# Two row tiles to one key/value instruction, with a newly stored order, in a fused attention and gated-MLP kernel

## The chip, the cores and the metric

The kernel runs on one core of one Trainium2 chip. The metric is the device time of one execution in microseconds, as the median of several runs; lower is better. One more execution is recorded by the hardware profiler, and everything said of instructions below comes from that record. The notes call the engines PE (TensorE, matrix products), ACT (ScalarE), DVE (VectorE), POOL (GpSimd) and SP (SyncE, which here issues nearly all DMAs).

## The reference

Input x has 2048 rows of 448 numbers in bf16. All weights are bf16.

```python
x = A_x
h  = x + _A_ref(_layernorm(x), A_wqkv, A_w_phi, A_wo)
h2 = h + _B_ref(_layernorm(h), B_w_gate, B_w_up, B_w_down)

# _A_ref: 16 heads of 28
q, k, v = split(x @ wqkv)
phi_q = concat(softmax(q @ w_phi), softmax(-(q @ w_phi)))
phi_k = concat(softmax(k @ w_phi), softmax(-(k @ w_phi)))
kv  = einsum("bhsf,bhsd->bhfd", phi_k, v)
z   = sum over s of phi_k
num = phi_q @ kv ;  den = phi_q @ z + 1e-6
out = (num / den) @ wo
# _B_ref
out = (sigmoid(x @ w_gate) * (x @ w_up)) @ w_down      # w_gate, w_up: 448 x 1792
```

The state kv is a sum over all 2048 rows, so every row's keys and values must be done before the first row's num can start.

## The kernel before

**Tiles.** The rows are 16 tiles of 128. The work goes by these tasks, named as in the code with the tile, pair or chunk behind the name:

- First layer norm, by tile: statistics `bst`, `agg`; the root `rstd` on POOL; the normalized tile `xn` on DVE or ACT. The transposed tile `xT` comes from PE for tiles 0 to 3 and from a DMA transpose of two tiles for the rest (line 628, issued by SP).
- Weights folded with w_phi: for keys `kT`, `WkT`, `wM1`, `W21` at the start; for queries two DMA transposes `wqT` (line 508), then `wM0` (line 562) and `W20`.
- Keys and values (line 644): one pair of products of 448 columns each takes turns on the two halves of PE's rows. It is two tasks, a first part of four steps (`pa`) and a second of three (`pb`), and fills one pair of PSUM banks. Before the change a pair is the keys and the values of one tile, for all tiles but the first two.
- Softmax of the keys, by tile: `ekp` and `ekm` (exponentials of both signs, ACT, lines 664 and 666), `v1` (values out of PSUM, ACT or DVE), `ss` (sums, DVE, line 685), `rs` (reciprocals, DVE, line 689), `phi` (the product, DVE or POOL, line 691). Then `kv` (PE, line 703) adds the tile to the state in bank 4, and `kvz` (DVE, line 758) takes the state out after tile 15.
- Queries by chunks of four tiles and two halves of the heads: `qa` and `q` (PE, line 743), `eqp` and `eqm` (ACT, line 753).
- Attention by tile: `num` (PE, line 779), `ocp` (ACT or DVE, out of PSUM). By pair of tiles on DVE: `rSm`, `rr`, `b`, `c`, `rd`, `o`, `od` (lines 795 to 826). The transpose `oT` is on PE for pair 0 and a DMA for the others. `woa` and `wo_` (PE, line 840) are the output product. For pair 0 the residual is added on PE (`wr`), and `hc`, `bst2`, `agg2` read PSUM; for the others `h` (line 870) adds it on DVE. Then `ve2`, `rstd2` (POOL, line 880), `hn` (DVE, line 884), `hP` and `hT`.
- MLP by chunks of 2, 4, 4, 4 and 2 tiles: `ga` and `gu` (PE, line 941, gate and up together), `sig` (ACT, line 950), `hh` (DVE, line 958), `dn` (PE, line 975), `fin` (DVE, line 982), `st` (the store, line 985). Tile 15 alone is split into two halves of 224 columns, `dn` 15 and `dn` 15,1.

**What sets the order.** Every task is one entry of a graph with its needs. The table ORDER holds, for every task, its number, its choice among the PSUM banks and its choice of engine. The tasks are issued on their engines in the order of the table, and each engine runs its own queue strictly in that order:

```python
for v in table.split():
    t = self.tasks[names[int(v) // 32]]
    t.eng = t.engs[int(v) % 4]
    ...
        t.got, gate = t.banks[int(v) // 4 % 8]
        for b in t.got:
            t.need += bank_until.get(b, [])
```

So a product whose banks were used before waits for the readers of their former content (`until`). Keys and values may use the bank pairs 0-1, 2-3 and 6-7. A second table, TURNS, adds needs by hand: an entry `(name, first)` makes `name` wait for `first` as well. Nearly all entries hold a POOL task back until a DVE task is done. A few products of zeros (`warm`, `fill`) run on PE while the first loads are under way.

Of the kernel before, what the change touches and what calls it, by code (L numbers as in the profile page):

```python
# [11 lines left out]
D = 448  # L12
H = 16
DH = 28
# [18 lines left out]
NFILL = 12  # L33
# [56 lines left out]
TURNS = [(('rstd', 4), ('xn', 3)), (('phi', 0), ('xn', 9)), (('phi', 4), ('xn', 12)), (('phi', 7), ('xn',  # L90
         15)), (('phi', 10), ('phi', 9)), (('phi', 14), ('phi', 13)), (('ve2', 2), ('hn', 3)), (('rstd2', 2),
         ('hn', 3)), (('ve2', 4), ('o', 5)), (('rstd2', 4), ('o', 5)), (('rstd2', 3), ('od', 5)), (('rstd2',
         5), ('od', 7))]
# [7 lines left out]
class _Graph:  # L101
# [29 lines left out]
    def opt(self, name):  # L131
        return name if name in self.tasks else None
# [180 lines left out]
def act_p(n):  # L313
    return 0.05 + n / 1200.0
# [14 lines left out]
def build(nc, A_x, A_wqkv, A_w_phi, A_wo, B_w_gate, B_w_up, B_w_down, out):  # L329
# [19 lines left out]
    with ExitStack() as es:  # L349
# [236 lines left out]
        VV = (0,)  # L586
        batches = [(0, 1), (1, 2), (2, 4), (4, 8), (8, 12), (12, 16)]
        for (a, z) in batches:
# [13 lines left out]
            for t in range(a, z):  # L602
                s = t % NXP
                free = opt(("xT", t - NXP if t - NXP in PE_X else (t - NXP) // 2 * 2))

                def f(e, t=t, s=s):
                    dst, src = xn_pad[:, s, :].rearrange("p (a n) -> p a n", a=2), lap(X(t))
                    if K.tasks[("xn", t)].eng == "act":
                        return e.activation(dst, src, ACT.Identity, bias=nm1[:, t:t + 1], scale=rs1[:, t:t + 1])
                    return e.tensor_scalar(dst, src, mv1[:, t, 0:1], rs1[:, t:t + 1], op0=ALU.subtract, op1=ALU.mult)  # L610
                task(("xn", t), None, dve(160), f, [("rstd", a), opt(("nm", a)), free],
                     engs=("dve",) if a < 4 else ("act", "dve"))
# [37 lines left out]
        for t in range(NT):  # L650
            if t in VV:
                both_ = [xT_of[t], xT_of[t + 1]]
                pair_of(("va", t), ("vb", t), [(t, Wv), (t + 1, Wv)], both_ + WV, [("v1", t), ("v1", t + 1)])
                pair_of(("pa", t), ("pb", t), [(t, Wk2), (t + 1, Wk2)], both_ + WK2,
                        [(n, u) for n in ("ekp", "ekm") for u in (t, t + 1)])
# [6 lines left out]
        for t in range(NT):  # L662
            s = t % NEK
            task(("ekp", t), "act", act_p(D), lambda e, t=t, s=s: e.activation(  # L664
                ek[:, s, 0, :], bank[got(k_at[t][0])[k_at[t][1]]][:, 0:D], ACT.Exp), [k_at[t][2], opt(("phi", t - NEK))])
            task(("ekm", t), "act", act_p(D), lambda e, t=t, s=s: e.activation(  # L666
                ek[:, s, 1, :], bank[got(k_at[t][0])[k_at[t][1]]][:, 0:D], ACT.Exp, scale=-1.0),
                [k_at[t][2], opt(("phi", t - NEK))])
            task(("v1", t), None, act_p(D), lambda e, t=t: copy(
                e, v1[:, t % NV, :, 0:DH], bank[got(v_at[t][0])[v_at[t][1]]][:, 0:D].rearrange("p (h d) -> p h d", d=DH)),  # L670
# [365 lines left out]
```

## Time and profile before

| what | value |
|---|---|
| median of 3 runs | 205.62 us (205.51 to 205.68) |
| the profiled execution | 205.42 us |
| its span, first to last instruction | 203.7 us |
| PE busy in the span | 195.8 us |
| DVE, ACT, POOL busy | 134.2, 94.6, 32.8 us |
| DMA | 16.94 MB |
| granted TensorE clock, mean | 0.999 |

The span is 1.7 us shorter than the execution that it is part of. "Busy" of PE is modelled from the starts of pipelined products, so two that overlap count once. A wait is put down to the instruction that released it.

### The profile page before, as it was taken

What the parts mean: (1) busy time and instruction counts of PE and PEld (TensorE: products, weight loads), DVE (VectorE), ACT (ScalarE), POOL (GpSimd) and SP (SyncE); (2) the same over time, 40 slices, a digit from 0 to 9 for tenths busy, and PEclk for the clock granted to TensorE, in tenths of its full rate; (3) what the DMA queues carried; (4) which work ended last, traced back from release to release, by engine and by line L of the source; (5) the groups of instructions that cost most, each with busy time, mean ns of one, the idle gap of its engine ahead of it and who ended that gap; (6) DMA issues with size and microseconds to landing.
All of it is one profiled execution on the core that took longest, in us unless ns stands there. A gap on an engine that the chain in (4) does not pass through costs nothing.

```text
span 203.7 us, 5394 instructions
## 1 busy us (share of the span) xinstructions
PE 195.8 (96%) x2276; PEld 109.5 (54%) x2276; DVE 134.2 (66%) x304; ACT 94.6 (46%) x169; POOL 32.8 (16%) x51
## 2 busy tenths in 40 slices
PE   7997999998889999999999999999999999999994
PEld 2543546555446985554445555454444555786553
DVE  2979989897999995789949846722455313541412
ACT  2699999999999553344031441202224400442000
POOL 5516936660000200003000100110000000000000
PEclk9999999999999999999999999999999999999999
DMA  5999696653045283501250020050020000200141
GB/s 144 313 271 149 173 194 159 187 198 93 3 103 145 80 93 79 140 0 43 51 116 3 0 53 3 5 121 3 0 74 3 2 3 0 69 3 0 34 158 59
DMA packets 35109, 16.94 MB, mean 83 GB/s; under 512 B 26828, under 2 KB 34060, under 8 KB 35084
## 3 DMA queue, kind: packets, MB, share of 16 engines
q1 hardware_dynamic: 34812, 16.36, 33.5%
q8 instruction: 18, 0.29, 0.6%
q10 hardware_dynamic: 272, 0.23, 0.3%
q14 instruction: 7, 0.06, 0.1%
HBM read 8.98 MB, written 1.84 MB: 53 GB/s over the span
## 4 chain that ended last, share of the span: by engine, by line
PE 86%; DMA 5%; DVE 3%; SPq 3%; issue 1%; ACT 0%; DVEq 0%
PE bank L941 42%; PE bank L975 21%; PE bank L644 8%; PE bank L743 5%; PE bank L840 5%; DMA WqT<-wq_raw 3%; SPq L468 3%; PE bank L703 2%; DMA wq_raw<-in_A_wqkv_dram 2%; PE bank L779 1%; SPq L508 1%; DVE o_pad L807 1%; DVE opm L432 1%; DVE st L865 1%; PE bank L562 1%
## 5 line engine op out<-in xcount | busy, mean ns | idle before, releaser
L941 PE MATMUL bank<-xnT,wu_sb 64*128 64x512 bf16 (+1 forms) x490 | 87.6, 333 | 0.0
L941 PE MATMUL bank<-xnT,wg_sb 64*128 64x512 bf16 (+1 forms) x490 | 87.5, 333 | 0.0
L950 ACT ACTIVATE sg_sb<-bank 128x512 f32<-128x512 f32 (+1 forms) x70 | 34.6, 511 | 81.4 <-PE bank L941 75.6
L958 DVE SCALAR_TENSOR_TENSOR hh<-sg_sb,bank 128x512 bf16<-128x512 f32 (+1 forms) x70 | 39.0, 575 | 30.3 <-ACT sg_sb L950 28.0
L941 PEld LDWEIGHTS bank<-xnT,wg_sb 64*128 64x128 bf16 x490 | 45.0, 94 | 20.8 <-issue 2.8
L941 PEld LDWEIGHTS bank<-xnT,wu_sb 64*128 64x128 bf16 x490 | 44.8, 94 | 13.9
L975 PE MATMUL bank<-wd_sb,hh 128*128 128x448 bf16 (+1 forms) x238 | 43.1, 342 | 0.0
L975 PEld LDWEIGHTS bank<-wd_sb,hh 128*128 128x128 bf16 x238 | 22.9, 98 | 20.1 <-DVE hh L958 0.4
L982 DVE SCALAR_TENSOR_TENSOR x_sb<-bank,x_sb 128x448 bf16<-128x448 f32 (+1 forms) x17 | 9.8, 594 | 24.6 <-PE bank L975 24.5
L644 PE MATMUL bank<-Wv,xnT 64*128 64x448 bf16 x112 | 21.9, 350 | 0.1
L644 PE MATMUL bank<-Wk,xnT 64*128 64x448 bf16 x112 | 21.7, 350 | 0.2
L691 POOL TENSOR_TENSOR phi<-ek,rsum 128x896 bf16<-128x896 bf16 x10 | 16.8, 1688 | 8.9 <-DVE xn_pad L610 4.7
L685 DVE TENSOR_REDUCE ssum<-ek 128x32 f32<-128x896 bf16 x16 | 16.6, 1069 | 0.8 <-ACT ek L664 0.7
L753 ACT ACTIVATE eq<-bank 128x1024 bf16<-128x1024 f32 x16 | 16.6, 1062 | 0.2
L880 POOL TENSOR_TENSOR rs<-rs,neghalf 128x2 f32<-128x2 f32 x8 | 5.6, 698 | 59.5 <-DVE rs L878 59.2
L743 PE MATMUL bank<-xnT,Wq 64*128 64x512 bf16 x112 | 14.3, 377 | 0.0
L840 PE MATMUL bank<-wo_sb,oT 64*128 64x448 bf16 x112 | 13.0, 350 | 0.6 <-DVE rs L878 0.6
L432 ACT CAST opm<-bank 128x960 bf16<-128x960 f32 x13 | 12.0, 972 | 1.4 <-PE bank L779 1.4
L644 PEld LDWEIGHTS bank<-Wk,xnT 64*128 64x128 bf16 x112 | 9.2, 94 | 5.9 <-PE bank L644 1.5
L644 PEld LDWEIGHTS bank<-Wv,xnT 64*128 64x128 bf16 x112 | 9.2, 94 | 5.0 <-ACT WkT L432 0.4
L870 DVE TENSOR_TENSOR x_sb<-bank,x_sb 128x896 bf16<-128x896 f32 x7 | 7.5, 1087 | 3.4 <-PE bank L840 3.4
L666 ACT ACTIVATE ek<-bank 128x448 bf16<-128x448 f32 x16 | 8.9, 563 | 0.9 <-PE bank L644 0.9
(92 smaller groups left out, 168.0 us busy)
## 6 DMA issues: line engine op xcount, KB each, us to landing
wu_sb<-in_B_w_up_dram SPq DMA_DIRECT2D x4, 448.0 KB, 4.1
wg_sb<-in_B_w_gate_dram SPq DMA_DIRECT2D x4, 448.0 KB, 3.9
out_dram<-x_sb SPq DMA_DIRECT2D x15, 112.0 KB, 1.8
wd_sb<-in_B_w_down_dram SPq DMA_DIRECT2D x7, 224.0 KB, 2.8
x_sb<-in_A_x_dram SPq DMA_DIRECT2D x2, 448.0 KB, 4.8
x_sb<-in_A_x_dram SPq DMA_DIRECT2D x3, 224.0 KB, 4.4
wq_raw<-in_A_wqkv_dram SPq DMA_DIRECT2D x4, 128.0 KB, 3.7
Wv<-in_A_wqkv_dram SPq DMA_DIRECT2D x2, 224.0 KB, 4.8
```

The costliest lines, as they stand in the source:

```text
L432: return e.copy(dst, src) if hasattr(e, "activation") else e.tensor_copy(dst, src)
L644: r = e.matmul(bank[bk][:, 0:D], lhsT=half(xnT, hi)[:, t, k, :], rhs=half(w, hi)[:, k, :], start=(i == 0), stop=(i == 6), tile_position=(6 ...
L685: task(("ss", t), "dve", dve(896), lambda e, s=s: e.tensor_reduce(ssum[:, s, :].rearrange("p (a h) -> p a h", h=2), ek[:, s].rearrange("p ...
L691: task(("phi", t), None, 1.68, lambda e, t=t, s=s: e.tensor_tensor(phi[:, t % NPHI, :, :, 0:DH, :].rearrange("p a g d h -> p (a g) d h"), ...
L743: r = e.matmul(bank[bb[j]], lhsT=half(Wq2, hi)[:, k, 2 * g:2 * g + 2].rearrange("p c d h -> p (c d h)"), rhs=half(xnT, hi)[:, 4 * c:4 * c ...
L753: task((key, gp, c), "act", act_p(1024), lambda e, gp=gp, c=c, sg=sg, nm=nm: e.activation(eq[c][:, sg, 2 * gp:2 * gp + 2, :], wide[got(nm) ...
L840: r = e.matmul(bank[bb[j]][:, 0:D], lhsT=half(oT, hi)[:, pr % NO, j, k, :], rhs=half(wo_sb, hi)[:, k, :], start=(i == 0 and not res), stop ...
L941: r = e.matmul(bank[b][:, 0:N], lhsT=half(w, hi)[:, k, fs], rhs=half(hnT, hi)[:, t0:t0 + n, k, :], start=(i == 0), stop=(i == 6), tile_pos ...
L950: task(("sig", f_, c), "act", act_p(N), lambda e, j=j, N=N, nm=nm: e.activation(sg_sb[:, j % NSG, 0:N], bank[got(nm)[0]][:, 0:N], ACT.Tanh ...
L958: task(("hh", f_, c), "dve", dve(N), lambda e, j=j, N=N, nm=nm, f_=f_, c=c: e.scalar_tensor_tensor(hhT[c % 2][:, f_, 0:N], sg_sb[:, j % NS ...
L975: r = e.matmul(bank[b][:, c0:c1], lhsT=hhT[c % 2][:, f_, o:o + P], rhs=wd_sb[:, f_, c0:c1], start=(f_ == 0), stop=(f_ == FT - 1))
L982: task(("fin",) + nm[1:], "dve", dve(c1 - c0), lambda e, nm=nm, tt=tt, pr=pr, c0=c0, c1=c1: e.scalar_tensor_tensor(X(tt)[:, c0:c1], bank[g ...
```

## The change

Keys and values are no longer paired within a tile. For every two tiles t and t+1 (t even) there is one pair of products with the values of both (`va`, `vb`) and one with the keys of both (`pa`, `pb`), as tiles 0 and 1 had it before. Where t is in PAIRED (2 to 12, that is tiles 2 to 13), one instruction over both banks does `ekp` for two tiles, one does `ekm`, one `v1`, one `ss`, one `rs`. `phi` and `kv` stay by tile, and tiles 0, 1, 14 and 15 stay single. A bank pair is now free when the one reader of both banks is done. Two needs that named `pb` by number now look the task up (`k_at`), and the unused branch SPLIT is gone. There are 14 fill products in place of 12.

ORDER is a new table for the whole program, and TURNS has 7 entries in place of 12. Cut to its core:

```diff
-NFILL = 12
+NFILL = 14
-TURNS = [(('rstd', 4), ('xn', 3)), (('phi', 0), ('xn', 9)), (('phi', 4), ('xn', 12)), (('phi', 7), ('xn',
-         15)), (('phi', 10), ('phi', 9)), (('phi', 14), ('phi', 13)), (('ve2', 2), ('hn', 3)), (('rstd2', 2),
-         ('hn', 3)), (('ve2', 4), ('o', 5)), (('rstd2', 4), ('o', 5)), (('rstd2', 3), ('od', 5)), (('rstd2',
-         5), ('od', 7))]
+TURNS = [(('phi', 3), ('phi', 2)), (('phi', 5), ('xn', 14)), (('phi', 8), ('phi', 9)), (('rstd2', 0), ('c',
+         3)), (('rstd2', 2), ('hn', 3)), (('rstd2', 4), ('od', 5)), (('rstd2', 6), ('hn', 10))]
...
-        VV = (0,)
+        VV = tuple(range(0, NT, 2))
+        PAIRED = (2, 4, 6, 8, 10, 12)
...
+                def keys(t=t, n=n):
+                    nm, j, _ = k_at[t]
+                    return wide[got(nm)[0]][:, j:j + n, 0:D]
+                task(("ekp", t), "act", act_p(n * D), lambda e, s=s, n=n, keys=keys: e.activation(
+                    ek[:, s:s + n, 0, :], keys(), ACT.Exp), [k_at[t][2]] + free)
+                task(("ekm", t), "act", act_p(n * D), lambda e, s=s, n=n, keys=keys: e.activation(
+                    ek[:, s:s + n, 1, :], keys(), ACT.Exp, scale=-1.0), [k_at[t][2]] + free)
+                task(("v1", t), None, act_p(n * D), lambda e, t=t, n=n: copy(
+                    e, v1[:, t % NV:t % NV + n, :, 0:DH],
+                    wide[got(v_at[t][0])[0]][:, v_at[t][1]:v_at[t][1] + n, 0:D].rearrange("p c (h d) -> p c h d", d=DH)),
...
+                task(("ss", t), "dve", dve(896 * n), lambda e, s=s, n=n: e.tensor_reduce(
+                    ssum[:, s:s + n, :].rearrange("p c (a h) -> p (c a) h", h=2),
+                    ek[:, s:s + n].rearrange("p c a (g d h) -> p (c a g) h d", g=2 * G, h=2), AX.X, ALU.add),
+                task(("rs", t), "dve", dve(256 * n), lambda e, s=s, n=n: e.reciprocal(rsum[:, s:s + n, :], ssum[:, s:s + n, :]),
```

What the new ORDER makes of the queues, where it differs most:

- SP: x of tiles 0 to 7 and the key weights first, as before; then the query weights `wq` stand ahead of the value weights `wv`, with x of tiles 8 to 11 between the `wq`; x of tiles 12 to 15 still stands last before the two transposes `wqT`.
- PE, first stage: the four `kT` stand together, the key products of tiles 0 to 3 come before the value products. From `wM0` on, pairs of `va` and `pa` alternate; `kv` goes two or three tiles at a time.
- After `kvz`: `num` 0, 2, 1, 4, 3, 6, 5, 7 among the queries of chunks 2 and 3; `ocp` 0 and 1 on DVE and 2 to 7 on ACT (before 0 and 3 on DVE).
- Pair 0 of the second layer norm: both `hc` are on DVE (before one was on ACT). The DVE queue is `hc` 1, `bst2` 0, `b` 3, `bst2` 1, `hc` 0, the two `agg2`, `c` 3, `h` 1, `hn` 1, `hn` 0, `h` 2, `hT`. `rstd2` 0 on POOL waits for `c` 3 (TURNS). On PE `woa` 2 and `wo_` 2 now stand ahead of `hP`. Fourteen `num` stand before the first `ga` (before: thirteen).
- The end of PE's queue is `dn` 10, 12, 11, 14, 15, 15,1, 13; before it was `dn` 12, 10, 13, 14, 11, 15, 15,1.

More of the change, by code (lines that the diff above doesn't have):

```diff
@@ L603, in build @@
                 s = t % NXP
-                free = opt(("xT", t - NXP if t - NXP in PE_X else (t - NXP) // 2 * 2))
+                free = None if t < NXP else ("xT", t - NXP if t - NXP in PE_X else (t - NXP) // 2 * 2)
                 def f(e, t=t, s=s):
@@ L652, in build @@
                 both_ = [xT_of[t], xT_of[t + 1]]
-                pair_of(("va", t), ("vb", t), [(t, Wv), (t + 1, Wv)], both_ + WV, [("v1", t), ("v1", t + 1)])
+                pair_of(("va", t), ("vb", t), [(t, Wv), (t + 1, Wv)], both_ + WV, [("v1", u) for u in ((t,) if t in PAIRED else (t, t + 1))])
                 pair_of(("pa", t), ("pb", t), [(t, Wk2), (t + 1, Wk2)], both_ + WK2,
-                        [(n, u) for n in ("ekp", "ekm") for u in (t, t + 1)])
+                        [(n, u) for n in ("ekp", "ekm") for u in ((t,) if t in PAIRED else (t, t + 1))])
                 for j in range(2):
@@ L663, in build @@
             s = t % NEK
[L664 to L670, printed above, removed]
-                [v_at[t][2], "v1one", opt(("kv", t - NV))], engs=("act", "dve"))
@@ L673, in build @@
-            if t in SPLIT:
-                task(("sa", t), None, 0.88, lambda e, t=t, s=s: e.tensor_tensor(
-                    half_s[:, t % NSA].rearrange("p (a n) -> p a n", a=4 * G),
-                    ek[:, s].rearrange("p a (g n) -> p (a g) n", g=2 * G)[:, :, 0:DH],
-                    ek[:, s].rearrange("p a (g n) -> p (a g) n", g=2 * G)[:, :, DH:2 * DH], ALU.add),
-                    [("ekp", t), ("ekm", t), opt(("ss", t - NSA))],
-                    engs=("pool", "dve"))
-                task(("ss", t), "dve", dve(448), lambda e, t=t, s=s: e.tensor_reduce(
-                    ssum[:, s, :].rearrange("p (a h) -> p a h", h=2),
-                    half_s[:, t % NSA].rearrange("p (a d h) -> p a h d", a=4 * G, h=2), AX.X, ALU.add),
-                    [("sa", t), opt(("rs", t - NEK))])
-            else:
-                task(("ss", t), "dve", dve(896), lambda e, s=s: e.tensor_reduce(
-                    ssum[:, s, :].rearrange("p (a h) -> p a h", h=2),
-                    ek[:, s].rearrange("p a (g d h) -> p (a g) h d", g=2 * G, h=2), AX.X, ALU.add),
-                    [("ekp", t), ("ekm", t), opt(("rs", t - NEK))])
@@ L689, in build @@
-            task(("rs", t), "dve", dve(256), lambda e, s=s: e.reciprocal(rsum[:, s, :], ssum[:, s, :]),
-                 [("ss", t), opt(("phi", t - NEK))])
+            n = 2 if t in PAIRED else 1
+            if t - 1 in PAIRED:
+                pass
+            else:
+                free = [opt(("phi", u - NEK)) for u in range(t, t + n)]
+                def keys(t=t, n=n):
[8 more added lines that the diff above has]
+                    wide[got(v_at[t][0])[0]][:, v_at[t][1]:v_at[t][1] + n, 0:D].rearrange("p c (h d) -> p c h d", d=DH)),
+                    [v_at[t][2], "v1one"] + [opt(("kv", u - NV)) for u in range(t, t + n)], engs=("act", "dve"))
+                task(("ss", t), "dve", dve(896 * n), lambda e, s=s, n=n: e.tensor_reduce(
+                    ssum[:, s:s + n, :].rearrange("p c (a h) -> p (c a) h", h=2),
+                    ek[:, s:s + n].rearrange("p c a (g d h) -> p (c a g) h d", g=2 * G, h=2), AX.X, ALU.add),
+                    [("ekp", t), ("ekm", t), opt(("rs", t - NEK)), opt(("rs", t - NEK + 1))])
+                task(("rs", t), "dve", dve(256 * n), lambda e, s=s, n=n: e.reciprocal(rsum[:, s:s + n, :], ssum[:, s:s + n, :]),
+                     [("ss", t)] + free)
@@ L691, in build @@
+            of = t - 1 if t - 1 in PAIRED else t
             task(("phi", t), None, 1.68, lambda e, t=t, s=s: e.tensor_tensor(
@@ L694, in build @@
                 rsum[:, s, :].rearrange("p (a h) -> p a h", h=2)[:, :, None, :].to_broadcast([P, 4 * G, DH, 2]), ALU.mult),
-                [("rs", t), ("ekp", t), ("ekm", t), opt(("kv", t - NPHI))], engs=("dve", "pool"))
+                [("rs", of), ("ekp", of), ("ekm", of), opt(("kv", t - NPHI))], engs=("dve", "pool"))
             def f(e, t=t):
@@ L707, in f @@
                 return r
-            task(("kv", t), "pe", 0.28, f, [("phi", t), ("v1", t), opt(("kv", t - 1)) or "kv0"], pace=1.9, rows=127)
+            task(("kv", t), "pe", 0.28, f, [("phi", t), ("v1", of), opt(("kv", t - 1)) or "kv0"], pace=1.9, rows=127)
         task("kv0", "pe", 0.22, lambda e: e.matmul(
@@ L718, in build @@
                  deps=([late[i - 2][0]] if i > 1 else []) + [
-                     ("kvz" if j < 4 else ("gu", 1 + 2 * j, 0)) if name[0] == "wd" else ("pb", 4 + 2 * j + (name[0] == "wu"))])
+                     ("kvz" if j < 4 else ("gu", 1 + 2 * j, 0)) if name[0] == "wd" else k_at[4 + 2 * j + (name[0] == "wu")][2]])
         WO_MOVES = [(0, 0, 112, 0, 0), (1, 0, 16, 0, 112), (1, 16, 96, 1, 0), (2, 0, 32, 1, 96), (2, 32, 80, 2, 0),
@@ L747, in build @@
                 deps = WQ2 + [xT_of[t] for t in range(4 * c, 4 * c + 4)]
-                deps.append(("pb", min(4 * c + 3, NT - 1)))
+                deps.append(k_at[min(4 * c + 3, NT - 1)][2])
                 task(nm, "pe", pes(4, 512), lambda e, f=f: f(e, steps=range(4)), deps,
@@ L887, in build @@
                     [("rstd2", pr), h_of.get(t)] + [d for d in hT_of.get(pr - NHP, [])])
-            qdone = [("q", gp, c) for gp in range(2)] + [("pb", NT - 1)]
+            qdone = [("q", gp, c) for gp in range(2)] + [k_at[NT - 1][2]]
             if pr in PE_O:
```

91 rows, old and new, of the table ORDER are left out of this document.

## The prediction

> **What bounds the kernel now.** I read the page's first part, then busy time by stages that I cut at the places where the kind of work changes, then PE's waits in each stage, and last the chain and the DMA view at both ends of the program.
>
> ```profile
> PE 195.8 (96%) x2276; PEld 109.5 (54%) x2276; DVE 134.2 (66%) x304; ACT 94.6 (46%) x169; POOL 32.8 (16%) x51
> ...
> core 0: us, PE busy (x) PEld busy (x) DVE busy (x) ACT busy (x) POOL busy (x), PEclk, DMA share, GB/s
> ...
> 6.50:18.10 11.60, 10.34 (x106) 5.46 (x106) 10.14 (x32) 10.81 (x24) 4.53 (x10) 1.00 1.15 256
> 18.10:46.50 28.40, 28.40 (x498) 15.90 (x500) 26.36 (x51) 26.41 (x50) 18.30 (x14) 1.00 0.70 175
> 46.50:64.80 18.30, 16.17 (x330) 8.83 (x330) 17.38 (x41) 17.62 (x22) 0.70 (x1) 1.00 0.35 92
> 64.80:77.60 12.80, 12.77 (x252) 11.29 (x245) 11.99 (x35) 6.96 (x17) 1.58 (x3) 1.00 0.54 85
> 77.60:184.70 107.10, 107.09 (x997) 57.09 (x998) 60.72 (x127) 30.78 (x57) 3.68 (x6) 1.00 0.14 35
> 184.70:200.80 16.10, 16.05 (x99) 9.40 (x98) 4.42 (x10) 0.76 (x4) 0.00 (x0) 1.00 0.21 66
> 200.80:203.70 2.90, 0.00 (x0) 0.00 (x0) 0.38 (x1) 0.00 (x0) 0.00 (x0) 0.91 0.24 72
> ```
>
> From 18.1 us on PE is the bound, at the full clock. In the key/value stage (18.1 to 46.5) it has no idle time at all, although ACT and DVE are at 93% there, and from 64.8 to 200.8 it misses 0.09 us. What can be won or lost lies in four places: how early PE can start its unbroken run (18.1), whether ACT and DVE still keep up until 46.5, the 2.13 us idle between 46.5 and 64.8, and the 2.9 us behind PE's last product. The change leaves the number of products as it was (two more fills run while PE waits for loads), so PE's own work cancels in the difference.
>
> PE's waits between 46.5 and 64.9, and the chain at the start and end:
>
> ```profile
> PE bank L779 <- DVE opm L432: 0.6, 2, 0.5
> PE bank L848 <- DVE oT L432: 0.6, 1, 0.6
> PE bank L840 <- DVE rs L878: 0.6, 1, 0.6
> PE bank L779 <- ACT opm L432: 0.3, 1, 0.3
> ...
> 10.50 1.39 SPq L508
> ...
> 12.00 6.05 DMA WqT<-wq_raw
> 18.05 0.05 issue
> 18.10 0.77 PE bank L562 x12
> ...
> 184.72 16.05 PE bank L975 x98
> 200.76 0.02 issue
> 200.79 0.39 DVE x_sb L982
> ```
>
> **a. The start.** PE's run begins when the second query transpose lands. The new SP queue puts the `wq` loads ahead of `wv`, so the transposes can be issued earlier than 10.50. But their packets stand behind all loads issued before them, and the bytes ahead are the same but for 84 KB (a 98 KB piece of `wo` gives way to one of 14 KB). The DMA engines run full from 6.5 to 16.6 (share 1.15). At the 256 GB/s of that stage 84 KB are 0.3 us. The view of 16 to 18 us, in 40 slices of 50 ns, shows one thing more:
>
> ```profile
> GB/s 231 225 174 251 195 210 230 195 195 128 118 51 31 15 0 0 0 0 0 10 5 10 10 5 10 10 10 10 5 15 5 15 5 10 26 246 266 297 297 287
> ...
> q8 instruction: 1, 0.02, 1.6%
> ```
>
> For about 1.1 us, from 16.6 to 17.7, nearly nothing moves, and only then does the transpose end. The second row, of the view of 12 to 16 us, is a read of instructions just ahead of it. Whether it falls there again cannot be read from the trace; PE's instruction count reaches that point at about the same time. I take -0.3 us, with bounds of -1.0 (the gap goes) and +0.3.
>
> **b. The key/value stage.** The 18 merged ACT instructions each replace two. Their pitch, start to start, and that of a longer one:
>
> ```profile
> 30.42 0.55 ACT L666 ACTIVATE ek<-bank 128x448 bf16<-128x448 f32 x1
> 30.85 0.55 ACT L664 ACTIVATE ek<-bank 128x448 bf16<-128x448 f32 x1
> ...
> 47.99 4.41 ACT L432 CAST opm<-bank 128x960 bf16<-128x960 f32 x5 [0.33 <-PE bank L779]
> ...
> 33.40 2.02 DVE L685 TENSOR_REDUCE ssum<-ek 128x32 f32<-128x896 bf16 x2
> ```
>
> Two singles take 2 x 0.43 = 0.86. Five of 960 columns end 4.41 after the first start; the last one's own 0.97 taken off leaves 4 pitches of 0.86 for 960 columns, so 896 columns take about 0.80. That saves 18 x 0.06 = 1.1 us of ACT. The sums save at most the start of one instruction, some 0.05 each, 0.3 us on DVE. None of it is on the path: PE has 28.40 us of work in 28.40. The price is that a reader holds both banks to its end. I walked PE's new queue with the durations of this trace from 18.1, and at each product that waits for banks set the reader's end beside it: `pa` 8 has its keys' banks 0.25 us before it comes up, `qa` 1,0 0.15, `pa` 12 0.25, `qa` 1,1 0.25, `va` 12 0.35. The last `phi` on DVE ends near 45.3 and its `kv` comes at 46.2. So all is in time, closely: 0. The bounds are 0 (PE cannot do its work faster) and +0.8 (five waits of 0.15, if two-bank instructions cost no less than two singles).
>
> The Trainium skill speaks for a larger saving (VectorE: DVE Perf Modes, "The TRN2 errata"): an instruction of ScalarE out of PSUM pays a fixed 172 cycles at 1.2 GHz, paid once for a large tile. By it the 18 would save 18 x 0.143 = 2.6 us of ACT; the rows show 1.1. It would change nothing in the sum, but make the third rival below less likely.
>
> **c. From `kvz` to the first `ga`.** These rows carry the walk:
>
> ```profile
> 44.82 1.71 PE L703 MATMUL bank<-v,phi 128*64 128x58 bf16 x96
> ...
> 46.57 0.64 DVE L758 TENSOR_TENSOR kvz<-bank,dmask 128x464 bf16<-128x464 f32 x1 [0.74 <-PE bank L703]
> ...
> 55.39 2.96 ACT L753 ACTIVATE eq<-bank 128x1024 bf16<-128x1024 f32 x3
> ...
> 56.47 1.74 PE L840 MATMUL bank<-wo_sb,oT 64*128 64x448 bf16 x14
> ...
> 58.71 1.16 DVE L865 BATCH_NORM_STATS2 st<-bank 128x6 f32<-128x448 f32 x2
> ...
> 61.64 0.73 DVE L884 TENSOR_SCALAR hn_pad<-x_sb,mv,rs 128x512 bf16<-128x512 bf16 x2
> ...
> 62.84 1.09 DVE L870 TENSOR_TENSOR x_sb<-bank,x_sb 128x896 bf16<-128x896 f32 x1
> ...
> 64.77 0.27 PE L941 MATMUL bank<-xnT,wu_sb 64*128 64x256 bf16 x1
> ...
> 61.67 0.23 PE bank L779 x16
> ```
>
> If the last `kv` ends at 46.5 in both, `num` 0 starts at 47.5 in both (it waits for `kvz` and for PE itself). Then the new queue waits at `num` 4 for `ocp` 0 (0.2), at `num` 6 for `ocp` 1 (0.65, both now on DVE one behind the other, 1.1 us each) and at `qa` 1,2 for `ocp` 3 on ACT (0.5). These are 1.35 us in place of the three waits for `opm` above (0.9); but the 0.6 at L848 goes, since `o` 0 is done at 54.1 and PE comes to it at 54.8. So `woa` 0 comes at 56.3 against 56.47. Behind it the second norm of pair 0 is longer: both `hc` on DVE (0.6 more), `b` 3 in between, and POOL's power waits for `c` 3 (0.6). `hn` 1 is done at 63.4, where before it was at 62.0. `woa` 1, `woa` 2 and their `num` fill most of that. Then `num` 11 waits for `h` 2 (1.09, from 63.8) and `ga` for the `hT` behind it on DVE: 65.2 against 64.77, with one `num` (0.23) more done. Net +0.2, bounds -0.8 and +1.0: eight waits guessed to 0.1 each.
>
> **d. The way into the MLP.** `ocp` 13, 8 and 11 stand on ACT directly ahead of the first `ga` that want their banks, 0.86 us apart, while a unit of chunk 0 takes 0.77: two waits of 0.17. Then `ga` 3,1 comes up near 77.2 and needs `hT` 2. Its `hn` 5 is done at 73.6, and a DMA transpose takes from its issue:
>
> ```profile
> xnT<-hn_pad SPq DMA_TRANSPOSE x7, 2.8
> ```
>
> That is 76.4. In the trace of before the same transpose landed just when PE came (77.57, 0.04 idle). Together +0.3, bounds 0 and +0.9. From there to 184.7 the new order has the same units with two to three units between a `ga` and the `hh` that frees its banks, as before: 0.
>
> **e. The end.** Before, PE ended with half a tile, and the last `fin` and store were of 224 columns. Now it ends with the whole tile 13:
>
> ```profile
> L982 DVE SCALAR_TENSOR_TENSOR x_sb<-bank,x_sb 128x448 bf16<-128x448 f32 x15 | 9.1, 621 | 20.8 <-PE bank L975 20.7
> ...
> L982 DVE SCALAR_TENSOR_TENSOR x_sb<-bank,x_sb 128x224 bf16<-128x224 f32 x2 | 0.8, 391 | 3.8 <-PE bank L975 3.8
> ...
> out_dram<-x_sb SPq DMA_DIRECT2D x15, 112.0 KB, 1.8
> ...
> out_dram<-x_sb SPq DMA_DIRECT2D x2, 56.0 KB, 1.5
> ```
>
> 0.62 - 0.39 = +0.23 on DVE, 1.8 - 1.5 = +0.3 for the store, nothing behind it: +0.5, bounds +0.3 and +0.6. This is the surest term.
>
> **Sum.** -0.3 + 0 + 0.2 + 0.3 + 0.5 = +0.7 us. The profiled execution took 205.42, so 206.1; the median of the runs lies 0.2 above it at 205.62, so **206.3 us**. A measurement of this kernel can tell about 0.2%, 0.4 us, from no change.
>
> **Rivals.**
>
> 1. *Faster, 204.9.* The gap in the DMA at 16.6 does not come again, because the transposes are issued earlier and the read of instructions falls elsewhere: PE starts 1.0 earlier, everything until 46.5 moves with it, and the new order wins 0.5 of the 2.13 us idle behind it in place of losing 0.2. -1.0 - 0.5 + 0.3 + 0.5 = -0.7. For it speaks that PE waited 1 us at 18.1 and for nothing else in that stage; against it that `xT` 4 is next in the same queue of transposes, and lets PE win only as much as it comes earlier too. It decides if the second `wqT` lands before 17.6 and `xT` 4 before 18.3.
> 2. *No difference, 205.6.* The order between 46.5 and 64.8 is better by 0.5 than my walk has it, and pays for the tail: -0.3 - 0.3 + 0.1 + 0.5 = 0. For it: only a third of the waits in that stretch need go.
> 3. *Slower by more, 207.5.* In the key/value stage ACT becomes the bound, since each reader now holds two banks and PE has three pairs for a queue of 0.15 to 0.35 us to spare: 0.8 there, a further 0.4 behind it as ACT enters the `num` stage late, with +0.7: +1.9. For it: ACT at 93%; against it: the 1.1 us that merging saves on ACT.
>
> That the change does not do what it says is out: the queues show the merged instructions.
>
> **Numbers.** My forecast 0.38, rival 1 0.22, rival 2 0.20, rival 3 0.20. So faster by over 0.2% 0.22, within 0.2% (205.2 to 206.0) 0.20, slower 0.58. The range takes the bounds of a and c to the one side, and those of b, c and d to the other without all at once: 204.5 to 208.0; the forecast's own is 206.0 to 207.0.
>
> **What would show it.** Right: `WqT` landing between 17.4 and 18.1, then no PE idle time until the last `kv`, 28.4 us later; `woa` 0 9.8 us behind that and the first `ga` 18.7; from PE's last product to the end 3.4 us in place of 2.9. Wrong: PE idle between 18 and 46; a first `ga` before 64; a transpose that lands before 17.

## The result: 0.84% slower, and the profile after

The changed kernel took 207.07 us (median of 17 runs, 205.79 to 207.91) against 205.18 of the kernel before (17 runs on the same chip, 204.48 to 205.88): a ratio of 1.0084, 95% interval 1.0066 to 1.0103 (the two medians alone give 1.0092, or 1.9 us). The profiled execution took 207.69, its span 205.8. In one experiment, the kernel before with halved fills, the profiled execution ran in a disturbed state at a lower clock; nothing is read from that profile.

First the page's busy times, then the view of busy time by stages, cut at the same events as before: the second `wqT` landed, the last `kv` ended, the first `ga` started, PE's last product ended.

```profile
PE 197.1 (96%) x2278; PEld 110.1 (53%) x2278; DVE 134.9 (66%) x292; ACT 93.1 (45%) x150; POOL 33.4 (16%) x52
```

```profile
core 0: us, PE busy (x) PEld busy (x) DVE busy (x) ACT busy (x) POOL busy (x), PEclk, DMA share, GB/s
6.50:18.30 11.80, 10.38 (x106) 5.42 (x105) 11.20 (x37) 10.45 (x20) 5.22 (x11) 1.00 1.15 225
18.30:46.80 28.50, 28.36 (x498) 15.78 (x500) 25.37 (x35) 25.09 (x34) 18.46 (x14) 1.00 0.78 192
46.80:66.70 19.90, 17.08 (x342) 8.79 (x343) 17.89 (x41) 18.68 (x23) 0.70 (x1) 1.00 0.30 80
66.70:202.50 135.80, 135.79 (x1320) 77.92 (x1320) 76.67 (x171) 37.59 (x76) 5.07 (x8) 1.00 0.17 42
202.50:205.80 3.30, 0.02 (x1) 0.00 (x0) 0.62 (x1) 0.00 (x0) 0.00 (x0) 1.00 0.20 70
```

The stage of keys and values is as long as before, with DVE 1.0 and ACT 1.3 us less busy. The stage that grew is the third: 19.9 us where it was 18.3, with 2.8 us of PE idle in place of 2.1. The rest of its growth is PE's own work, 17.08 us in place of 16.17, in part the one `num` more that now stands ahead of the first `ga`. The waits of PE from 18 to 80 us (total, times, longest), and then the chain through that place (start, length), say on what:

```profile
PE bank L837 <- DMA oT<-o_pad: 1.5, 1, 1.5
PE bank L559 <- DMA WqT<-wq_raw: 1.2, 1, 1.2
PE bank L776 <- DVE opm L429: 0.6, 2, 0.5
PE bank L740 <- ACT opm L429: 0.3, 1, 0.3
PE bank L938 <- ACT opm L429: 0.2, 1, 0.2
```

```profile
58.76 4.35 DMA oT<-o_pad
63.11 0.04 issue
63.15 0.93 PE bank L837 x8
...
66.71 1.35 PE bank L938 x21
```

One wait is new: `woa` 2 (line 837, which was 840) waits 1.5 us for the DMA transpose `oT` 2, which took 4.35 us from issue to landing. In the kernel before the same transpose took 2.71, and the read nearest to it started 3.48 us behind its issue. Look at the DMA view of the 1.2 us from 60.9 on:

```profile
GB/s 120 86 572 17 0 0 0 0 0 0 0 0 149 90 60 179 119 179 239 149 149 149 149 60 209 209 119 209 209 209 239 239 329 329 329 359 329 388 329 389
...
q8 instruction: 1, 0.02, 5.3%
```

A read of instructions, 16 KB, starts there (at 60.98, and takes 1.02 us), just as the last packets of the transpose go out. The events in the trace show that a transpose lands in 16 parts. For `oT` 2, counted from its issue, 15 parts landed by 2.73 us; the read started at 2.22 and the sixteenth part landed at 4.35.

To compare the kernels, the marks of the steps, in us (starts of the products in the timeline, the last `kv` and PE's end by their ends):

| execution | first `pa` of the long run | last `kv` | `woa` 0 | first `ga` | PE's end | span |
|---|---|---|---|---|---|---|
| before | 18.81 | 46.52 | 56.47 | 64.77 | 200.76 | 203.7 |
| after | 19.21 | 46.80 | 56.21 | 66.71 | 202.53 | 205.8 |
| after, once more | 19.05 | 46.64 | 56.05 | 66.46 | 202.28 | 205.5 |
| after, merged instructions split | 18.97 | 46.73 | 56.14 | 65.40 | 201.22 | 204.5 |

### The profile page after: what moved, and what is told of

The parts are those of the page before. It is cut to its first block, busy times and chain, and to the rows that moved or that the text cites. A ratio compares the mean times of both kernels' runs of the same rounds, so it can differ in the third digit from the quotient of the medians.

```text
span 205.8 us, 5368 instructions
## 1 busy us (share of the span) xinstructions
PE 197.1 (96%) x2278; PEld 110.1 (53%) x2278; DVE 134.9 (66%) x292; ACT 93.1 (45%) x150; POOL 33.4 (16%) x52
## 4 chain that ended last, share of the span: by engine, by line
PE 83%; DMA 7%; SPq 4%; ACT 2%; DVE 2%; issue 0%
PE bank L938 42%; PE bank L972 21%; PE bank L643 8%; PE bank L740 5%; PE bank L837 4%; SPq L465 4%; DMA x_sb<-in_A_x_dram 3%; PE bank L700 2%; DMA xnT<-xn_pad 2%; DMA oT<-o_pad 2%; ACT opm L429 2%; PE bank L776 1%; ACT eq L750 0%; DVE o_pad L804 0%; DVE x_sb L979 0%
## 5 line engine op out<-in xcount | busy, mean ns | idle before, releaser
L947 ACT ACTIVATE sg_sb<-bank 128x512 f32<-128x512 f32 (+1 forms) x70 | 34.1, 512 | 81.5 <-PE bank L938 77.9
L681 DVE TENSOR_REDUCE ssum<-ek 128x64 f32<-128x1792 bf16 (+1 forms) x10 | 16.2, 1630 | 1.7 <-ACT ek L672 1.2
L750 ACT ACTIVATE eq<-bank 128x1024 bf16<-128x1024 f32 x16 | 16.0, 1039 | 0.9 <-PE bank L740 0.8
L429 ACT CAST opm<-bank 128x960 bf16<-128x960 f32 x14 | 13.0, 982 | 2.5 <-PE bank L776 2.5
L643 PE MATMUL bank<-Wv,xnT 64*128 64x448 bf16 x112 | 13.1, 350 | 0.1
L643 PE MATMUL bank<-Wk,xnT 64*128 64x448 bf16 x112 | 12.8, 350 | 0.2
L589 DVE BATCH_NORM_STATS2 st<-x_sb 128x6 f32<-128x448 bf16 x16 | 9.1, 608 | 1.1 <-DMA x_sb<-in_A_x_dram 1.1
L837 PEld LDWEIGHTS bank<-wo_sb,oT 64*128 64x128 bf16 x112 | 5.4, 94 | 7.3 <-DMA oT<-o_pad 1.6
L871 DVE BATCH_NORM_STATS2 st<-x_sb 128x6 f32<-128x448 bf16 x14 | 8.3, 614 | 0.0
```

The costliest lines, as they stand in the source:

```text
L429: return e.copy(dst, src) if hasattr(e, "activation") else e.tensor_copy(dst, src)
L643: r = e.matmul(bank[bk][:, 0:D], lhsT=half(xnT, hi)[:, t, k, :], rhs=half(w, hi)[:, k, :], start=(i == 0), stop=(i == 6), tile_position=(6 ...
L681: task(("ss", t), "dve", dve(896 * n), lambda e, s=s, n=n: e.tensor_reduce(ssum[:, s:s + n, :].rearrange("p c (a h) -> p (c a) h", h=2), e ...
L750: task((key, gp, c), "act", act_p(1024), lambda e, gp=gp, c=c, sg=sg, nm=nm: e.activation(eq[c][:, sg, 2 * gp:2 * gp + 2, :], wide[got(nm) ...
L837: r = e.matmul(bank[bb[j]][:, 0:D], lhsT=half(oT, hi)[:, pr % NO, j, k, :], rhs=half(wo_sb, hi)[:, k, :], start=(i == 0 and not res), stop ...
L947: task(("sig", f_, c), "act", act_p(N), lambda e, j=j, N=N, nm=nm: e.activation(sg_sb[:, j % NSG, 0:N], bank[got(nm)[0]][:, 0:N], ACT.Tanh ...
```

## The experiments

Two theories stood against each other. Theory 1: PE's own instruction read holds the transpose back, and the new order has put `woa` 2 where it has no slack for that (slack is the time between the landing and the moment at which PE comes to the product). The rival: the two loads of `wd` that SP issues 1.3 and 1.9 us behind the transpose do it. Other runs take the terms of the sum one by one.

**The instruction read: PE's instruction count changed.** Three kernels change only the fill products at the start.

```diff
-NFILL = 14
+NFILL = 6          # and fills 6 to 13 taken out of ORDER
```

> The kernel after with 6 fill products in place of 14, so PE has 16 instructions fewer (8 weight loads, 8 products) ahead of everything else. Theory 1: the 1.51 us that PE idles at 61.6 come from a read of 16 KB of PE's instructions that starts at 60.98, 0.1 us ahead of the last packets of the transpose oT 2, and holds one of its 16 parts back (15 landed at 61.33 to 61.49, one at 63.11). PE runs about 36 instructions a us there, so the read comes about 0.4 us later, behind those packets: oT 2 lands 2.7 us after its issue in place of 4.35, PE waits for it under 0.2 us, and the time falls by about 1.4 us to 205.7. Rival: the two loads of wd issued 1.3 and 1.9 us behind the transpose hold its last part back; then the landing stays 4.3 us after the issue and the time stays at 207.1. At the start the read that fell at 15.46 comes later by up to 0.9 us; if it is what makes the DMA pause from 16.1 to 17.25, the pause moves with it.

207.75 us, ratio to before 1.0131 [1.0102, 1.0161]. The transpose did as theory 1 says: the read started 3.63 us behind its issue, it landed at 2.73, and PE has no wait for `oT` from 18 to 80 us. But the time did not fall: the first `ga` came 18.67 us behind the last `kv`, as without the late part, and the edit cost elsewhere. The last `kv` ended at 47.61 (after: 46.80), and behind the first `ga` it took 1.3 us more. These are its windows of the start, the clock being the last column but two:

```profile
4.00:6.50 2.50, 1.10 (x10) 0.76 (x9) 2.50 (x8) 0.40 (x1) 1.04 (x3) 1.00 1.05 270
6.50:9.00 2.50, 2.50 (x26) 2.28 (x26) 2.50 (x6) 2.12 (x6) 2.01 (x6) 0.67 0.95 215
9.00:12.00 3.00, 2.33 (x21) 1.66 (x20) 2.97 (x12) 1.94 (x4) 0.93 (x3) 0.50 1.15 339
12.00:15.00 3.00, 2.93 (x21) 1.05 (x21) 2.83 (x9) 1.40 (x2) 0.92 (x2) 0.63 1.23 172
```

Without the later fills PE rests for 1.4 us before 6.5 us, and the granted clock of these windows falls to 0.50 to 0.67 (the trace has it at 0.5 from 7.4 to 14.2 us; the windows that hold more than that show a mean). That is not the whole cost in the timed runs: three of the six had a mean clock of 0.997 to 1.0 and took 207.47 to 208.00 all the same. In the profiled one the next read met `hT` 2 (4.60 us), for which PE waited 1.1 us at 78.

```diff
-e.matmul(bank[5], lhsT=warm[:], rhs=warm[:, None, :].to_broadcast([P, 4, P]), ...)
+[e.matmul(bank[5][:, 128 * c:128 * (c + w)], lhsT=warm[:], rhs=warm[:, None, :].to_broadcast([P, w, P]), ...)
+ for c, w in ((0, 2), (2, 2))][-1]
```

> The kernel after with each of its 14 fill products cut into two of half the width: the same PE time, 28 instructions more, so every later read of instructions comes earlier. Theory 1 (the read holds the transpose back): near oT 2 the read comes 0.7 to 1.9 us earlier, at 59.1 to 60.3; before 59.9 it misses the packets (oT 2 lands 2.7 us after its issue, time about 205.7), between 59.9 and 61 it still holds one part back but by less, since it ends sooner (2.7 to 3.7 us, time 205.7 to 206.7). Rival (the loads of wd): 4.3 us as before, time 207.1. At the start the read comes near 14 us; if it makes the pause at 16.1, the pause goes or moves, and the second query transpose lands up to 1 us earlier than 18.28.

207.17 us, ratio 1.0105 [1.0081, 1.0129]: a miss for the sizes given. The read again started 2.22 us behind the issue of `oT` 2, which landed at 4.34; PE waited 1.5 us. 28 instructions did not take the read out of the transpose.

```diff
- for c, w in ((0, 2), (2, 2))][-1]
+ for c, w in (((0, 2), (2, 1), (3, 1)) if i < 11 else ((0, 2), (2, 2)))][-1]
```

> The kernel after with its 14 fill products cut into 39 parts of the same total width, 50 instructions of PE more ahead of everything. In after, in the kernel with 28 more and in the one with the new tail the read of PE's instructions started 2.22 us behind the issue of oT 2, at the end of its packets, and one part landed 1.7 us behind the 15 others; with 16 fewer it started 3.6 us behind and the transpose took 2.73. Theory 1 (the read is asked for by PE's instruction count and held back the transpose because it was asked for while that was under way): 50 instructions earlier are 1.4 us or more, before the issue of oT 2 at 58.7; then oT 2 lands 2.7 us after its issue, PE waits for it under 0.2 us, and the time is 205.7 (the read may meet oT 1 in its place, packets to 57.9, at 0.4 us). Rival (the read is asked for by something else near the transpose, and moves with it): 4.3 us and 207.1 as after.

208.27 us, ratio 1.0139 [1.0088, 1.0191]. Half of the expectation held: the read started 0.50 us ahead of the issue of `oT` 2, which landed 2.73 behind it. The time rose all the same. Other reads now met other transposes, and PE stopped once at a place that has none to wait for. Its waits and its chain:

```profile
PE bank L938 <- DMA xnT<-hn_pad: 1.0, 1, 1.0
...
PE bank L776 <- issue: 0.8, 1, 0.8
PE bank L837 <- DMA oT<-o_pad: 0.6, 1, 0.6
```

```profile
49.24 0.54 PE bank L776 x25
49.77 0.81 issue
...
71.24 4.25 DMA oT<-o_pad
...
167.70 4.74 DMA xnT<-hn_pad
```

The transposes that PE waits for are now `oT` 3 (4.25 us, a read 2.18 behind its issue) and `hT` 7 (4.74, a read 1.22 behind). The late landing goes with the read, wherever that falls. The 0.8 us at 49.8 (the second line of the waits) fall inside one `num`, behind its ninth product. The 25 products in the chain are one `num` of 16 and 9 of the next. The kernel puts its waits only ahead of a task, so PE does not wait for another engine or a DMA there; what holds it the profile does not show.

**The loads behind the transpose.** `wd` 2 and `wd` 3 stand behind `hT` 1 in SP's queue.

```diff
-SP: ... oT1, oT2, wd2, wd3, oT3, hT1, hT2 ...
+SP: ... oT1, oT2, oT3, hT1, wd2, wd3, hT2 ...
```

> The kernel after with the two loads of wd that SP issues 1.3 and 1.9 us behind oT 2 moved behind the transpose hT 1, so nothing is queued behind oT 2. Theory 1 (the read alone holds one of the 16 parts): the read starts at 60.98 and ends near 62.0; the last part lands behind it, 62.3 to 62.5 if the loads' packets then stood in its way as well, 63.1 if not; PE waits 0.7 to 1.5 us and the time is 206.4 to 207.1. Rival (the loads of wd alone do it): oT 2 lands 2.7 us after its issue, PE waits under 0.2 us, time 205.6.

208.02 us, ratio 1.0133 [1.0093, 1.0173]. The rival falls. With no load behind it the transpose is as late as ever, and PE waits 0.9 us more at another place (for `hT` 2, which lands at 78.65; PE waits from 77.82 to 78.74; the second line of the waits below). `hT` 2 is queued behind the moved loads, but a read also starts 0.29 us ahead of its issue; which of the two delays it is not shown. The chain and the waits:

```profile
58.10 4.26 DMA oT<-o_pad
```

```profile
PE bank L837 <- DMA oT<-o_pad: 1.4, 1, 1.4
PE bank L938 <- issue: 1.1, 2, 0.9
```

**All transposes together.** Behind 50 us the other 13 profiled executions hold 182 DMA transposes. This is worked out from their issue, the landings of their parts, and the starts of the instruction reads:

| transposes | count | us from issue to last landing |
|---|---|---|
| a read starts 1.0 to 2.6 us behind the issue | 23 | 4.2 to 4.8 |
| no read in that stretch, issue itself at most 1.4 us long | 148 | 2.7 to 2.8, one 3.1 |
| no read in that stretch, issue drawn out to 1.7 to 2.5 us | 11 | 3.0 to 4.2 |

Where the read starts 2.18 us or more behind the issue (17 of the 23) only the last part is late; where it starts 1.0 to 1.9 behind (6) all 16 are. The 11 with a drawn-out issue are not free of reads: in each of them a read starts between 0.3 us ahead of the issue and 0.8 behind it. But each also follows a transpose that a read had made late, so which of the two draws the issue out is not shown.

**Why the old order did not pay.** The kernel before with more instructions ahead, first 24, then 14:

```diff
+ for c, w in ((0, 2), (2, 2))][-1]                                    # 24 more
+ for c, w in (((0, 2), (2, 2)) if i < 7 else ((0, 4),))][-1]          # 14 more
```

> The kernel before with each of its 12 fill products cut into two of half the width, 24 instructions more. Theory 1: the read of instructions that stood at 62.31, 0.8 us behind the landing of oT 2, comes about 0.7 us earlier or more and can meet the transpose's packets (60.0 to 61.0); then one part of oT 2 lands 1 to 1.7 us behind the others, PE waits for it, and the kernel before becomes slower by 0.3 to 1.4 us, 205.5 to 206.6, though nothing else is changed. If the read is only queued behind the loads of wd there, it stays and the time stays at 205.2. Rival: no change in oT 2 (2.71 us from issue to landing) and in the time (205.2), as the fills are PE time that nothing waits for.

205.21 us, ratio 1.0007 [0.9992, 1.0022]: no change in time, so the loss of 0.3 to 1.4 us that theory 1 allowed for did not come; whether the read met `oT` 2 in the timed runs is not known.

> The kernel before with 7 of its 12 fill products cut into two halves: 14 instructions of PE more ahead of everything, between the kernel before (read 3.5 us behind the issue of oT 2) and the one with 24 more (0.6 us behind it). Theory 1 (the old order has slack where the new one has none): if the read now meets oT 2, it lands 4.3 us behind its issue, near 63.1, but woa 2 stands behind hP in that order and PE comes to it at 63.0, so PE waits at most 0.3 us, and the time stays within 0.3 us of before, 204.9 to 205.3; and no two groups of times 1 us apart. Rival (a read that meets oT 2 costs the old order as much): PE waits 1.4 us and the times go to 206.4.

205.34 us, ratio 1.0010 [0.9984, 1.0036]. Here the read met it. The DMA view from 58.5 to 64 us, PE's waits from 58 to 70, and the chain at this place:

```profile
oT<-o_pad SPq DMA_TRANSPOSE x1, 4.2
```

```profile
PE bank L840 <- DVE rs L878: 0.6, 1, 0.6
```

```profile
59.02 4.20 DMA oT<-o_pad
63.21 0.05 issue
63.26 0.93 PE bank L840 x8
```

The transpose took 4.2 us (the read 1.81 behind its issue), and PE shows no wait for it: `woa` 2 stands behind `hP` there and comes up at 63.2, just as the transpose lands. The first `ga` comes 18.35 us behind the last `kv`, in before 18.25. So in this place the old order has the slack, all of which the late part uses up, and the read costs it 0.1 us at most.

**Merging alone.** The new order with every merged instruction issued as two.

```diff
-lambda e: e.activation(ek[:, s:s + n, 0, :], keys(), ACT.Exp)
+lambda e: [e.activation(ek[:, s + i:s + i + 1, 0, :], keys()[:, i:i + 1], ACT.Exp) for i in range(n)][-1]
 # the same for ekm, v1, ss, rs
```

> The kernel after with its own order, pairs and waits, but each merged instruction (both exponentials, values, sums, reciprocals of tiles 2 to 13) issued as two of one tile each, behind one another in the same place. Theory of the prediction (merging saves 0.06 us per ACT pair, 0.05 to 0.1 per DVE pair, and none of it is on the path): ACT gets 1.1 us busier, DVE about 0.9 (6 x 0.13 for reciprocals, 6 x 0.12 for sums come out of the rows of after), PE still has no idle time between its run's start and the last kv, time within 0.3 us of after (207.0). Rival (merging is what keeps ACT or DVE up with PE in this stage): PE idles there by 0.3 to 1 us, time 207.3 to 208.

207.01 us, ratio 1.0089 [1.0063, 1.0114]: the same as after. From 18.2 to 46.7 us PE has 28.48 us of work in 28.50, with ACT busier than in after:

```profile
18.20:46.70 28.50, 28.48 (x498) 15.66 (x500) 25.76 (x47) 26.20 (x50) 18.54 (x14) 1.00 0.74 191
```

What merging saves is hidden; the rival falls. This profiled execution (206.20 us) escaped the read, which started 2.92 us behind the issue of `oT` 2. It shows what the new order does without the late part. From the DMA view of 58 to 64 us and the chain of 57 to 67 us:

```profile
oT<-o_pad SPq DMA_TRANSPOSE x1, 2.7
```

```profile
62.21 1.82 ACT opm L429 x2
64.02 0.49 ACT xnT L429
64.51 0.87 ACT opm L429
65.39 0.01 issue
65.40 1.68 PE bank L938 x27
```

The chain into the first `ga` now runs over ACT's `ocp`, and no longer over the transpose.

**Fewer fills, and after once more.**

```diff
-NFILL = 14
+NFILL = 12
```

> The kernel after with 12 fill products, as the kernel before had, in place of 14: 4 instructions of PE fewer, the order otherwise that of after. Theory 1: the read asked for by PE's instruction count comes 0.1 us later, and the one that holds back oT 2 stands at the end of that transpose's packets; so more executions escape it than with 14 (4 of 17 then lay at 205.8 to 206.0, the others at 206.6 to 207.9). Median between 206.0 (most escape) and 207.0 (as before); in the profiled execution either the read starts 2.2 us behind the issue of oT 2, oT 2 lands 4.3 behind it and the first ga comes near 66.5, or it starts later, oT 2 lands 2.7 behind its issue and the first ga comes near 65.3. Rival (the two fills cost or save something by themselves): a change of the start by more than 0.3 us with oT 2 as in after.

207.11 us, ratio 1.0087 [1.0054, 1.0121]. Its ten times fall in two groups: 205.42, 205.68, 205.68, and seven from 206.68 to 208.34. The profiled one (206.93) is of the second: the read 2.22 behind the issue, the transpose 4.26. Three of ten escape by this reading, four of 17 with 14 fills: no clear gain, where more escapes were expected.

> The kernel after once more, unchanged, for a second profiled execution of it. Theory 1: its time follows from the read alone. If the read starts 2.2 us behind the issue of oT 2, that lands 4.3 us behind it, PE waits 1.4 to 1.5 us and the execution takes 206.6 to 207.9; if the read comes later, oT 2 lands 2.7 behind, PE does not wait, and it takes 205.8 to 206.3. Rival: the time goes with the start (WqT landing 17.8 to 18.3) or the clock, and not with oT 2.

207.46 us: the read 2.21 behind the issue, the transpose 4.26, PE's wait 1.4 us. Its first `ga` comes 19.82 us behind the last `kv`, in after 19.91, and in the execution that escaped 18.67. After's 17 runs show the same two groups: four at 205.79 to 206.01, thirteen at 206.61 to 207.91. That the lower group is the one that escapes was not seen in after itself. It rests on the one escaped profile (206.20) and on the eight profiles of the new order in which `oT` 2 was late, all of which took 206.74 us or more.

**The tail and the start.**

```diff
-PE: dn 10, 12, 11, 14, 15, 15,1, 13
+PE: dn 10, 12, 11, 13, 14, 15, 15,1      # fin and st in that order
```

> The kernel after with the end of PE's queue as dn 10, 12, 11, 13, 14, 15, 15,1 in place of 10, 12, 11, 14, 15, 15,1, 13, and the residual additions and stores in that order, so the last ones are of 224 columns again. Theory: from PE's last product to the end of the span 2.9 us in place of 3.27, time lower by 0.3 us: 206.8. Rival: the stores queue on SP and the end stays at 3.3 us, no change (207.1). The wait for oT 2 is untouched (1.5 us) in both.

206.88 us, ratio to before 1.0085 [1.0061, 1.0109]; the intervals of this ratio and of after's overlap, so the time alone does not show the 0.3. The profile does. Its last addition, ahead of it PE's end, in a span of 204.7:

```profile
201.77 0.02 issue
201.80 0.39 DVE x_sb L979
```

From PE's end to the end of the span it is 2.92 us, in after 3.27.

```diff
-SP: ... wq3, wq2, x8, wq0, wq1, wv1, wv0, x12 ...
+SP: ... wv1, wv0, wq3, wq2, x8, wq0, wq1, x12 ...
```

> The kernel after with the two loads of wv (224 KB each) back ahead of the four of wq (128 KB each) in SP's queue, as in the kernel before. In after the DMA moved 2.73 MB between 4 and 14.5 us, before 2.93; the rate falls where the loads of 128 KB are issued 0.5 to 0.6 us apart. Theory (SP's issue holds the DMA back there): the wq land later but the queue stays full, the second query transpose lands 0.2 to 0.4 us earlier than 18.28 and the time falls by as much, to 206.8. Rival (the start differs between executions by as much, 18.28, 18.02, 17.78 in three kernels that have the same queue): landing anywhere from 17.8 to 18.3, time within 0.2 us of after.

206.84 us, ratio 1.0076 [1.0059, 1.0094]; `WqT` landed at 17.50, the first `pa` of the long run came at 18.47. That is no verdict. Executions with after's own SP order have this product between 18.46 (12 fills) and 19.21 (after), and the kernel of the next run, with `wv` first again, has it at 19.01. The start moves by more than the edit.

> The kernel after with 12 fills, the tail of the new-tail kernel (tile 13 ahead of tiles 14 and 15) and wv ahead of wq on SP. Theory: the parts add up, 0.3 for the tail and 0.2 for wv, and whatever the fills bring: 206.5 where the read still holds oT 2 back, 205.2 where not, against 205.1 of before. Rival (start and tail are hidden by something): 207.0.

206.63 us, ratio 1.0060 [1.0037, 1.0083]; two of 12 runs at 205.10 and 205.47, the rest 206.26 and up. In its profile the read came 2.59 behind the issue and the transpose took 4.62. The parts add to some 0.4, and it still does not reach the kernel before.

## Why the prediction was right or wrong

The direction was right and the time in the range, but 207.07 is 0.8 above the forecast of 206.3 and just outside the forecast's own 206.0 to 207.0. The change itself is +1.9 us (from 205.18), where +0.7 was forecast. The measured time lies nearer to rival 3's 207.5, but by luck of the number alone: PE is idle for 0.1 us in the key/value stage, where rival 3 wanted 0.8. What made up most of the excess, a DMA transpose held back by an instruction read, was in neither the forecast's walk nor a rival's. By the steps:

**a, the start (-0.3).** Measured +0.40 in the profiled execution (18.81 to 19.21). With after's SP order the first `pa` lies anywhere from 18.46 to 19.21 (before 18.81, the second variant of before 19.00), so neither sign is shown, and the bounds of -1.0 and +0.3 were about as wide as the scatter. `WqT` landed at 18.28, outside the 17.4 to 18.1 that were to show the step right. The premise that the bytes ahead set the landing was not borne out: up to 14.5 us the DMA moved 3.48 MB in before and 3.38 in after, and with after's own SP order it moved 3.50 in the kernel with 12 fills. The gap came again, as rival 1 had to fear: a read of instructions starts in the transposes `WqT` in all profiles, at 15.0 to 16.5 us, and in seven of them, before among them, the second `WqT` lands 2.09 to 2.14 us behind its start. No run had the read elsewhere, so what it costs there is open.

**b, the key/value stage (0).** Right. From the first `pa` to the last `kv` it is 27.59 us against 27.71, and PE is idle for only 0.1 us there. The size of the saving held as well. Two merged exponentials in after, their start times 0.80 apart as estimated:

```profile
29.53 0.91 ACT L672 ACTIVATE ek<-bank 128x896 bf16<-128x896 f32 x1
30.33 0.92 ACT L674 ACTIVATE ek<-bank 128x896 bf16<-128x896 f32 x1
```

Two singles were 0.86, so an instruction spared is 0.06 us. The Trainium skill (VectorE: DVE Perf Modes, "The TRN2 errata") has a fixed 172 cycles at 1.2 GHz, which would be 0.14; the measurement decides against that for back-to-back instructions here. The split kernel shows that neither figure reaches the path. Rival 3 is out.

**c, from `kvz` to the first `ga` (+0.2).** This is the term that failed, by size and not by sign. The forecast was `woa` 0 9.8 us behind the last `kv` and the first `ga` 18.7 behind. Measured: 9.41 and, where the read is escaped, 18.67. In the two profiles of after it is 19.91 and 19.82. Against 18.25 of before, and less the 0.23 of the one `num` more, the term is +0.2 without the late part, as forecast, and +1.3 to +1.4 with it. That the part without it came out is partly luck: up to `woa` 0 the waits for `ocp` were 0.15, 0.48 and 0.30 in place of 0.2, 0.65 and 0.5, and from there to the first `ga` it took 9.26 us in place of 8.9, two errors of 0.4 that cancel. The step that failed is the walk over `woa` 2: it took 2.7 us for the transpose because before shows 2.71. The new order leaves `woa` 2 at 61.64 (where `num` 10 ends in after) with a transpose due at 61.5. In the old order a landing at 63.2 was still in time (the kernel before with 14 instructions more); the new order left 0.2 us.

Of the costs of an instruction read the Trainium skill says (Runtime: NRT & Kernel Launch, "Instruction fetch mechanics") that PE's sequencer fetches 16 KiB, 256 instructions, at a time by its own DMA queue and that this is "mostly hidden". The sizes agree: 18 reads for 4659 instructions of PE. In after PE itself mostly hides it: three reads start in the key/value stage, where PE is idle for 0.1 us. The transpose that a read meets is not spared: it lands 1.4 to 2 us later.

**d, the way into the MLP (+0.3).** Two waits for `ocp` of 0.17 were forecast; one of 0.2 is there, ahead of the first `ga` (line 938), and so within the stretch of c. For `hT` 2 no wait was forecast and none came. From the first `ga` to PE's end it is 135.82 against 135.99, with one `num` of 0.23 less to do: +0.06.

**e, the tail (+0.5).** +0.36 (3.27 against 2.91), and the tail experiment takes it back (2.92). Of the two parts the addition was right (0.62 in place of 0.39); the store added 0.1, not 0.3.

**The sum.** The escaped execution stands at 206.20, 0.8 above the 205.42 of before; the forecast was +0.7. That these agree is luck in part: by the terms it is +0.16 for a, +0.05 for b, +0.19 for c, +0.06 for d and +0.36 for e, where -0.3, 0, +0.2, +0.3 and +0.5 were forecast. The +0.8 by which the median exceeds the forecast is the late part of one transpose (1.2 us, from 18.67 to 19.91), in three executions of four if the two groups are read so, less the 0.44 by which the 17 runs of before lie under the three it was made against.

## What to carry to other kernels

When an order is tightened, look at what else may be late, not only at how late it was in one trace: a wait that now ends with a DMA transpose within 0.2 us has spent its slack. Look for the instruction reads in the DMA view beside every transpose that the path depends on, and keep about 2 us of other work between its normal landing and its reader. A saving on an engine that does not bound its stage is worth nothing, and the order it came with is what is measured.

## What the runs showed of the hardware that was not expected

A 16 KB read of PE's instructions takes 0.9 to 1.8 us on its queue, about 1.0 in most cases. A DMA transpose in which one started 1.0 to 2.6 us behind the issue landed 1.4 to 2 us late: 23 of 23, with 4.2 to 4.8 us against 2.7 to 2.8 for 147 of the other 159. In 16 of them the read starts 2.18 to 2.22 us behind the issue of the transpose, although PE's count of instructions differs between the kernels, so it seems to be asked for earlier and let in when the transpose's packets are out; that was not shown. And with 8 fill products fewer at the start, 1.4 us of rest for PE, the granted clock was 0.5 from 7.4 to 14.2 us in the profiled execution; in three of that kernel's six runs the mean clock was below 0.993, in the other three 0.997 to 1.0.
